# Weight transfers on ScalarE's queue, and moved sums and splits, in a one-core kernel of attention and two MLPs

## The chip, the core and the metric

The program runs on one core of a Trainium2 chip. The metric is the device time of one execution, in microseconds, lower is better. The kernel before was timed three times: median 1686.81 us (1684.53 to 1688.54).

## What is computed

```python
def sm_attn(qq, kk, vv):                         # softmax attention, scale 1/8
    ...
p_packed = sm_attn(p, k, v)                      # p: 32 packed queries a head
out = sm_attn(q, p_packed, p_packed)             # q, k, v: 8 x 8 x 576 x 64
x = out.transpose(0, 2, 1, 3).reshape(4608, 512)
h = x @ w_in1;  x = (h * sigmoid(h)) @ w_out1    # 512 -> 2048 -> 512
h = x @ w_in2;  g = h * clip(h + 3, 0, 6) / 6
out = g @ w_out2                                 # 512 -> 2048 -> 512
```

The two weight pairs arrive as 8-byte floats and are turned into fp32 on the core.

## The kernel before, in words

**Blocks.** The 4608 tokens go through attention and the first MLP in nine blocks (`block`, j = 0 to 8) of 512 columns. A block has 16 steps f, one for each 128 hidden units. In step f TensorE makes `hidden` (12 matmuls in block 0), ScalarE applies Silu (L828) and rounds the result to `gh` (L835), VectorE takes the rest `gl` (L836): every fp32 factor is a sum of a high and a low part, and a product is three matmuls. Then `projects(f - 2)` adds 12 matmuls. Attention for later blocks is spread between these matmuls by `Plan`, which releases a step when its place and its waiting time have come. Every engine runs its list strictly in order.

**Block 0 and `Feed`.** Block 0 also converts the weights of the first MLP. There are 32 pieces (keys), 16 of w_in and 16 of w_out in turn, two for each step f. `advance` number i does, in this order: one `load` (L1215, `load_raw`, L143: a 512 KB transfer into one of four `raw` buffers), `keep()` (stores of finished pieces to DRAM), `conv_end` of key i - 2 (ScalarE's cast L195 makes the high part, L196 the low one: VectorE for w_in, GpSimd for w_out), `conv_add` of key i - 1 (GpSimd, L182) and `conv_bits` of key i (VectorE, L176 and L177). `begin` (ScalarE, L170 and L171, tile `cr`) needs the piece's transfer to have landed. In block 0 `advance` runs after `split_g` and after `projects`, `begin` in the middle of `hidden` and of `projects`. Since an `advance` loads one piece, in block 0 the piece that `advance` i loads is key i + 1, and the `begin` that follows is the one of key i + 1.

**Who issues transfers.** SyncE (SP) issues the loads of k, q, v, p and `raw` in program order; an issue waits until the buffer is free. ScalarE issues the stores of pieces (L189) and the later loads of pieces: `next_in` (L216), `next_out` (L228) and `Prep` (L257, L301 to L303). An issue on ScalarE that has to wait holds up all that stands behind it there. Each transfer uses one of eight semaphores (DMAHW0 to 7), and its issue waits for the transfer that had that one before.

**`Prep`** converts the second MLP's weights in blocks 1 to 8, a piece of work at each call of `step`. Only block 1's first call starts it.

**The second MLP** (`Second`) works on six groups of 768 columns with a scheme of seven products in place of eight. `hidden` makes products k of hidden pieces f; `after` adds them (`hu` L1020, `hv` L1023); `gate` (L1007) makes g. For every odd f, `t1` (L1077, VectorE) and `split` follow 3 and 4 products later; `split` is ScalarE's rounding L1099 and VectorE's rest L1100. `project` runs 28 steps of 12 matmuls; `split` and `sums` prepare coming steps, and `next(self.prep)` does the sums and splits of the next group's x (`x_steps`) at even steps from 4. Weights come from DRAM through a ring of `WS` = 7 buffers `ws` (L942), loaded by SP.

Of the kernel before, what the change touches and what calls it, by code (L numbers as in the profile page):

```python
# [8 lines left out]
F32 = mybir.dt.float32  # L9
I32 = mybir.dt.int32  # L10
U32 = mybir.dt.uint32
F32R = mybir.dt.float32r
# [6 lines left out]
def tile_pack_attention_two_mlps(ctx: ExitStack, tc, q, k, v, p, w_in1, w_out1, w_in2, w_out2, out):  # L19
# [8 lines left out]
    nc = tc.nc  # L28
# [102 lines left out]
    WO = 3  # L131
    made = {}
    raws = {}
    kept = []

    def half_w(kind, f):
        if kind == "in":
# [4 lines left out]

    def load_raw(key, src):  # L143
        raw = wp.tile([P, 2 * T], I32, tag="raw", name="raw", bufs=RAW)
        nc.sync.dma_start(out=raw.rearrange("p (a f) -> p a f", a=src.shape[1]), in_=src)
        raws[key] = raw

    def win_src(w, f):
# [42 lines left out]
    def conv_end(key):  # L191
        kind, f = key
        v = raws.pop(key)
        w = half_w(kind, f)
        nc.scalar.copy(out=w[:, 0], in_=v)  # L195
        (nc.vector if kind == "in" else nc.gpsimd).tensor_sub(out=w[:, 1], in0=v, in1=f32(w[:, 0]))  # L196
        made[key] = w
        if kind == "in":
            kept.append((piece_in(f), f32(w).rearrange("p n (c f) -> p n c f", c=KC)))
        elif f % 2:  # L200
            kept.append((w1o[f].rearrange("n p f -> p n f"), f32(w)))

    def piece_in(f):
        return w1i[f // GF][:, :, :, f % GF, :].rearrange("c p n f -> p n c f")
# [13 lines left out]
                nc.scalar.dma_start(out=f32(t).rearrange("p n (c f) -> p n c f", c=KC), in_=piece_in(key[1]))  # L218
            have_in[key] = t

    projected = [-1]

    def next_out():

        while want_out and not kept and projected[0] >= NF - 2 and (want_out[0][0] * NF + want_out[0][1]) // 2 <= (projected[0] + 1) // 2 - 1 + WO:
            j, f = want_out.pop(0)
            t = half_w("out", f)
            nc.scalar.dma_start(out=f32(t), in_=w1o[f].rearrange("n p f -> p n f"))  # L228
            have_out[j, f] = t
# [7 lines left out]
    class Prep:  # L237
# [28 lines left out]

        def all(self):
            self.load(0)
            yield
            for u, (kind, f, h) in enumerate(self.units):  # L270
                key = "p", u
                c = self.pool.tile([P, 8, P], F32, tag="c8", name="c8")
                hi = self.pool.tile([P, S7, P], F32, tag="hi7", name="hi7")
                conv_begin(key, self.room)
                yield
                yield
                conv_bits(key)
                yield
                if u + 1 < len(self.units):
                    self.load(u + 1)  # L280
                yield
                x, r = (t.rearrange("p (n r f) -> p n r f", n=2, r=2) for t in raws.pop(key))
                a = c[:, 0:4].bitcast(I32)
                a = a.rearrange("p (n r) f -> p n r f", n=2) if kind == "in" else a.rearrange("p (r n) f -> p n r f", n=2)
                nc.gpsimd.tensor_add(out=a, in0=x, in1=r)
                yield

                nc.vector.tensor_add(out=c[:, 4], in0=c[:, 2], in1=c[:, 3])
                nc.vector.tensor_sub(out=c[:, 6], in0=c[:, 0], in1=c[:, 2])
                nc.vector.tensor_sub(out=c[:, 5], in0=c[:, 4], in1=c[:, 0])  # L290
                nc.vector.tensor_sub(out=c[:, 7], in0=c[:, 1], in1=c[:, 5])
                yield
                nc.scalar.copy(out=hi[:, 0:2].bitcast(F32R), in_=c[:, 0:2])
                nc.scalar.copy(out=hi[:, 2:7].bitcast(F32R), in_=c[:, 3:8])
                yield
                nc.gpsimd.tensor_sub(out=c[:, 0:2].bitcast(F32R), in0=c[:, 0:2], in1=hi[:, 0:2])
                nc.gpsimd.tensor_sub(out=c[:, 3:8].bitcast(F32R), in0=c[:, 3:8], in1=hi[:, 2:7])
                yield
                yield
                to = w2[kind][f].rearrange("s p f -> p s f")  # L300
                nc.scalar.dma_start(out=to[:, :, h * P:(h + 1) * P], in_=hi)  # L301
                nc.scalar.dma_start(out=to[:, 0:2, (2 + h) * P:(3 + h) * P], in_=c[:, 0:2])
                nc.scalar.dma_start(out=to[:, 2:7, (2 + h) * P:(3 + h) * P], in_=c[:, 3:8])  # L303
# [602 lines left out]
    ROW = {1: 0, 2: 1, 4: 2, 5: 3, 6: 4, 7: 5, 3: 6}  # L906
    ORDER_P = (1, 5, 6, 3, 7, 2, 4)
    FD = HF // 2
    WS = 7

    class Second:
        def __init__(self):
# [40 lines left out]
        def x_steps(self, n):  # L953

            xr = self.right.tile([P, KC, 2 * N], F32, tag="xr", name="xr")
            at_, end = 2 * N * n, 2 * N * (n + 1)
            o = 0
            while at_ < end:
                j, c0 = divmod(at_, T)
                m = min(end - at_, T - c0)  # L960
                nc.sync.dma_start(out=xr[:, :, o:o + m], in_=x1d[j][:, :, c0:c0 + m].rearrange("c p t -> p c t"))
                at_, o = at_ + m, o + m
            yield
            b = {(i, k): xr[:, 2 * i:2 * i + 2, k * N:(k + 1) * N] for i in range(2) for k in range(2)}
            e = [self.right.tile([P, 2, N], F32, tag=f"xe{i}", name=f"xe{i}") for i in range(3)]
            nc.vector.tensor_sub(out=e[0], in0=b[1, 1], in1=b[0, 1])
            nc.vector.tensor_sub(out=b[0, 1], in0=b[0, 1], in1=b[0, 0])
            yield
            nc.vector.tensor_sub(out=e[1], in0=b[1, 1], in1=b[0, 1])
            nc.vector.tensor_sub(out=e[2], in0=b[1, 0], in1=e[1])  # L970
            yield
            for k, v in (1, b[0, 0]), (6, e[1]), (5, b[0, 1]), (7, e[0]), (2, b[1, 0]), (4, e[2]), (3, b[1, 1]):
                t = self.right.tile([P, 2, 2, N], F32R, tag=f"xc{k}", name=f"xc{k}")
                nc.scalar.copy(out=t[:, 0], in_=v)
                nc.vector.tensor_sub(out=t[:, 1], in0=v, in1=f32(t[:, 0]))
                self.x[k] = t
                yield
# [10 lines left out]
        def hidden(self, n):  # L988
# [25 lines left out]
            def after(f, k):  # L1014
                if k == 1:
                    h1[f] = small("h1")
                    nc.scalar.copy(out=h1[f], in_=X[f])
                elif k == 6:
                    hu[f] = small("hu")
                    nc.vector.tensor_add(out=hu[f], in0=h1[f], in1=Y[f])  # L1020
                elif k == 7:
                    hv[f] = small("hv")
                    nc.vector.tensor_add(out=hv[f], in0=h1[f], in1=Y[f])  # L1023
                    nc.vector.tensor_add(out=hv[f], in0=hv[f], in1=Z[f])
                    act(f, (1, 1), hv[f])
                elif k == 2:
                    act(f, (0, 0), X[f])
                elif k == 4:
                    nc.vector.tensor_add(out=h1[f], in0=h1[f], in1=Y[f])
                    act(f, (1, 0), h1[f])  # L1030
                elif k == 3:
                    nc.vector.tensor_add(out=hu[f], in0=hu[f], in1=Z[f])
                    act(f, (0, 1), hu[f])
                    if f % 2:
                        soon(3, lambda: self.t1(f // 2))
                        soon(4, lambda: self.split(f // 2))

            for fd in range(FD):
                for part in ((0, 0), (0, 1), (1, 0), (1, 1)):
# [43 lines left out]
        def sums(self, s):  # L1083
# [8 lines left out]
            elif k == 4:  # L1092
                nc.vector.tensor_sub(out=t, in0=b21, in1=t)

        def split(self, s):
            if s < FD * S7:
                t = self.left.tile([P, 2, 2, N], F32R, tag="ro", name="ro", bufs=4)
                v = self.operand(s)
                nc.scalar.copy(out=t[:, 0], in_=v)  # L1099
                nc.vector.tensor_sub(out=t[:, 1], in0=v, in1=f32(t[:, 0]))  # L1100
                self.ro[s] = t

        def project(self, n):
            X, Y, Z = [], [], []
# [21 lines left out]
            for s in range(FD * S7):  # L1126
# [15 lines left out]
                self.sums(s + 4)  # L1142
                if s + 3 >= FD:
                    self.split(s + 3)
                if self.prep and s % 2 == 0 and s >= 4:
                    next(self.prep, None)
                yield
            if self.prep:
# [41 lines left out]
    class Feed:  # L1190
# [19 lines left out]
        def advance(self):  # L1210

            i, n = self.at, len(self.keys)
            if i > n + 1:
                return
            if self.loaded < i + self.ahead:  # L1215
                self.load()
            keep()
            if i >= 2:
                conv_end(self.keys[i - 2])
            if 1 <= i <= n:  # L1220
                conv_add(self.keys[i - 1])
            if self.begun == i:
                self.begin()
            if i < n:
                conv_bits(self.keys[i])
            self.at += 1
# [94 lines left out]
    for j in range(NBLK):  # L1321
# [44 lines left out]
        def nxt(f, full, j=j):  # L1366
            if j == 0:
                if full:
                    feed.advance()
                    calls[0] += 1  # L1370
                    if 12 <= calls[0] < 16:
                        next_in()
                else:
                    feed.begin()
            else:
                if j >= B - 1 or full:
                    prep.step()
                if full and j == B:
                    mlp2.begin_step()
# [52 lines left out]
```

## Time and profile before

| what | us |
|---|---|
| median of three runs | 1686.81 |
| the profiled execution's own time | 1691.33 |
| its span, first to last instruction | 1689.5 |
| TensorE (matmuls) busy | 1570.1 (93%) |
| VectorE busy | 1039.1 (62%) |
| ScalarE busy | 804.9 (48%) |
| GpSimd busy | 216.8 (13%) |

The profile is of one execution, 4.5 us longer than the median. An engine's busy time does not say that it sets the pace: a queue can be blocked without being busy, and issuing a transfer is not counted as busy. So a stage is read from what its engines wait for. "gh" rows (L835) mark the steps f of a block, since there is one of them in each step. A row of the timeline gives start, duration, engine, line, operation, output and inputs; in brackets how long the engine had been idle and what ended it. SPq and ACTq are the issues of transfers on SP and ScalarE. A row of windows gives the window and its length, then the busy time of PE, PEld (weight loads), DVE, ACT and POOL with the count of instructions, the granted clock of TensorE, the busy share of the DMA engines and GB/s. A row of waits gives the waiting instruction, what ended its wait, the us in total, the number of waits and the longest.

### The profile page before, as it was taken

What the parts mean: (1) busy time and instruction counts of PE and PEld (TensorE: products, weight loads), DVE (VectorE), ACT (ScalarE), POOL (GpSimd) and SP (SyncE); (2) the same over time, 40 slices, a digit from 0 to 9 for tenths busy, and PEclk for the clock granted to TensorE, in tenths of its full rate; (3) what the DMA queues carried; (4) which work ended last, traced back from release to release, by engine and by line L of the source; (5) the groups of instructions that cost most, each with busy time, mean ns of one, the idle gap of its engine ahead of it and who ended that gap; (6) DMA issues with size and microseconds to landing.
All of it is one profiled execution on the core that took longest, in us unless ns stands there. A gap on an engine that the chain in (4) does not pass through costs nothing.

```text
span 1689.5 us, 23588 instructions
## 1 busy us (share of the span) xinstructions
PE 1570.1 (93%) x8396; PEld 1343.7 (80%) x8396; DVE 1039.1 (62%) x1750; ACT 804.9 (48%) x1356; POOL 216.8 (13%) x188
## 2 busy tenths in 40 slices
PE   5877899889999899999989999999999999999997
PEld 3655656667676677767868999999999999999997
DVE  5645455465556555554343479569578678677675
ACT  4756345555555455555444345345345344444443
POOL 2443311111111021112213000000000000000000
PEclk9999899899999899999999999999999999999999
DMA  7786676776769665766698687787787887887875
GB/s 192 239 254 192 217 213 184 220 209 187 194 181 242 190 195 139 208 218 204 191 311 250 195 274 243 253 294 249 252 294 249 260 286 249 274 271 251 257 252 154
DMA packets 409749, 388.01 MB, mean 230 GB/s; under 512 B 156192, under 2 KB 282144, under 8 KB 409632
## 3 DMA queue, kind: packets, MB, share of 16 engines
q1 hardware_dynamic: 271264, 252.25, 49.6%
q10 hardware_dynamic: 138368, 134.24, 25.6%
q8 instruction: 68, 1.11, 0.3%
q14 instruction: 49, 0.40, 0.1%
HBM read 324.53 MB, written 61.87 MB: 229 GB/s over the span
## 4 chain that ended last, share of the span: by engine, by line
PE 55%; DVE 16%; ACT 13%; DMA 8%; issue 3%; POOL 2%; ACTq 1%; SPq 1%; DVEq 0%; POOLq 0%
PE acc L843 5%; PE b L1137 5%; PE acc L844 5%; PE b L1138 5%; PE acc L845 5%; PE b L1136 5%; PE b L1058 4%; PE b L1060 4%; PE b L1059 4%; PE hps L820 3%; ACT hr L1004 3%; DVE g L1007 3%; PE hps L822 3%; PE hps L821 3%; DVE ro L1100 2%
## 5 line engine op out<-in xcount | busy, mean ns | idle before, releaser
L1058 PE MATMUL b<-xc,ws 128*128 128x384 f32 x672 | 229.4, 341 | 8.0 <-DVE hu L1020 8.0
L1137 PE MATMUL b<-ro,ws 128*128 128x384 f32 x672 | 227.1, 338 | 6.2 <-DVE ro L1100 6.2
L1138 PE MATMUL b<-ro,ws 128*128 128x384 f32 x672 | 225.9, 336 | 0.0
L1136 PE MATMUL b<-ro,ws 128*128 128x384 f32 x672 | 225.8, 336 | 0.0
L1060 PE MATMUL b<-xc,ws 128*128 128x384 f32 x672 | 225.1, 335 | 0.0
L1059 PE MATMUL b<-xc,ws 128*128 128x384 f32 x672 | 224.8, 335 | 0.0
L836 DVE TENSOR_TENSOR gl<-hps,gh 128x512 fp32r<-128x512 f32 x144 | 99.1, 688 | 201.0 <-ACT gh L835 201.0
L1099 ACT CAST ro<-g 128x768 fp32r<-128x768 f32 x168 | 137.3, 835 | 116.9 <-DVE g L1089 34.9
L1100 DVE TENSOR_TENSOR ro<-g,ro 128x768 fp32r<-128x768 f32 x168 | 158.0, 953 | 23.7 <-ACT ro L1099 21.0
L1058 PEld LDWEIGHTS b<-xc,ws 128*128 128x128 f32 x672 | 126.2, 188 | 13.5 <-DVE hu L1020 13.4
L1137 PEld LDWEIGHTS b<-ro,ws 128*128 128x128 f32 x672 | 126.3, 188 | 9.7 <-DVE ro L1100 9.7
L828 ACT ACTIVATE hps<-hps 128x512 f32<-128x512 f32 x144 | 84.1, 584 | 95.6 <-PE hps L822 70.2
L1059 PEld LDWEIGHTS b<-xc,ws 128*128 128x128 f32 x672 | 126.3, 188 | 0.0
L1138 PEld LDWEIGHTS b<-ro,ws 128*128 128x128 f32 x672 | 126.3, 188 | 0.0
L1136 PEld LDWEIGHTS b<-ro,ws 128*128 128x128 f32 x672 | 126.3, 188 | 0.0
L1060 PEld LDWEIGHTS b<-xc,ws 128*128 128x128 f32 x672 | 126.1, 188 | 0.0
L843 PE MATMUL acc<-gh,wr 128*128 128x512 f32 x288 | 120.5, 418 | 0.9 <-ACT gh L835 0.9
L843 PE MATMUL acc<-gh,wo 128*128 128x512 f32 x288 | 117.9, 409 | 2.9 <-ACT gh L835 2.9
L844 PE MATMUL acc<-gl,wr 128*128 128x512 f32 x288 | 115.3, 400 | 0.3 <-DVE gl L836 0.2
L844 PE MATMUL acc<-gl,wo 128*128 128x512 f32 x288 | 114.2, 397 | 0.9 <-DVE gl L836 0.8
L845 PE MATMUL acc<-gh,wr 128*128 128x512 f32 x288 | 114.6, 398 | 0.0
L845 PE MATMUL acc<-gh,wo 128*128 128x512 f32 x288 | 113.8, 395 | 0.0
(262 smaller groups left out, 3046.3 us busy)
## 6 DMA issues: line engine op xcount, KB each, us to landing
ws<-w2in SPq DMA_DIRECT2D x336, 256.0 KB, 3.9
ws<-w2out SPq DMA_DIRECT2D x336, 256.0 KB, 3.5
wi<-w1i ACTq DMA_DIRECT2D x80, 512.0 KB, 4.8
wo<-w1o ACTq DMA_DIRECT2D x64, 512.0 KB, 4.7
x1d<-x SPq DMA_DIRECT2D x18, 512.0 KB, 3.2
raw<-in_moe_w_in_dram SPq DMA_DIRECT2D x16, 512.0 KB, 5.2
raw<-in_moe_w_out_dram SPq DMA_DIRECT2D x16, 512.0 KB, 4.7
w1i<-win ACTq DMA_DIRECT2D x16, 512.0 KB, 5.3
```

What stands on the lines that cost most here:

```text
L836: nc.vector.tensor_sub(out=gl, in0=g, in1=f32(gh))
L843: mm(acc[e], lhsT=w[:, 0, s], rhs=gh, start=first, stop=False)
L844: mm(acc[e], lhsT=w[:, 0, s], rhs=gl, start=False, stop=False)
L845: mm(acc[e], lhsT=w[:, 1, s], rhs=gh, start=False, stop=last)
L1058: mm(ps, lhsT=wh, rhs=xs[k][:, 0, c], start=first, stop=False, skip_group_check=True)
L1059: mm(ps, lhsT=wh, rhs=xs[k][:, 1, c], start=False, stop=False, skip_group_check=True)
L1060: mm(ps, lhsT=wl, rhs=xs[k][:, 0, c], start=False, stop=last, skip_group_check=True)
L1099: nc.scalar.copy(out=t[:, 0], in_=v)
L1100: nc.vector.tensor_sub(out=t[:, 1], in0=v, in1=f32(t[:, 0]))
L1136: mm(acc[i], lhsT=wh, rhs=ro[:, 0, f], start=first, stop=False, skip_group_check=True)
L1137: mm(acc[i], lhsT=wh, rhs=ro[:, 1, f], start=False, stop=False, skip_group_check=True)
L1138: mm(acc[i], lhsT=wl, rhs=ro[:, 0, f], start=False, stop=last, skip_group_check=True)
```

## The change

1. `load_raw` issues on SP only while `early` holds (the part ahead of block 0, five pieces); the other 27 pieces are issued on ScalarE.
2. The low part of a w_in piece (VectorE) is made one `advance` later from i = 6 on.
3. In block 0 `next_in` runs at calls 20 to 23 of `advance` instead of 12 to 15.
4. `next_out` goes by what held at its previous call, so its loads come one step f later.
5. `Prep` begins five calls later, and its tile `hi7` has two buffers.
6. In the second MLP the ring has `WS` = 6 buffers; `t1`, the rounding and the rest follow 2, 3 and 5 products after the odd f; the sums of x are spread over two more steps, and `next(self.prep)` runs at steps 1 to 3, 8 to 11, 16 to 19 and 24 to 27.

```diff
 def load_raw(key, src):
-        nc.sync.dma_start(out=raw..., in_=src)
+        (nc.sync if early[0] else nc.scalar).dma_start(out=raw..., in_=src)
...
 def conv_end(key):
         nc.scalar.copy(out=w[:, 0], in_=v)
-        (nc.vector if kind == "in" else nc.gpsimd).tensor_sub(out=w[:, 1], in0=v, in1=f32(w[:, 0]))
         made[key] = w
         if kind == "in":
-            kept.append((piece_in(f), ...))
-        elif f % 2:
-            kept.append((w1o[f]..., f32(w)))
+            lows.append((v, w, piece_in(f)))
+        else:
+            nc.gpsimd.tensor_sub(out=w[:, 1], in0=v, in1=f32(w[:, 0]))
+            if f % 2:
+                kept.append((w1o[f]..., f32(w)))
+
+    def conv_low():
+        while lows:
+            v, w, to = lows.pop(0)
+            nc.vector.tensor_sub(out=w[:, 1], in0=v, in1=f32(w[:, 0]))
+            kept.append((to, ...))
...
-    projected = [-1]
+    projected = [-1, -1]
 def next_out():
-        while want_out and not kept and projected[0] >= NF - 2 and ... <= (projected[0] + 1) // 2 - 1 + WO:
+        now, projected[1] = projected[1], -1 if kept else projected[0]
+        while want_out and now >= NF - 2 and ... <= (now + 1) // 2 - 1 + WO:
...
 class Prep: def all(self):
             self.load(0)
-            yield
+            for _ in range(6):
+                yield
...
-                hi = self.pool.tile([P, S7, P], F32, tag="hi7", name="hi7")
+                hi = self.pool.tile([P, S7, P], F32, tag="hi7", name="hi7", bufs=2)
...
-    WS = 7
+    WS = 6
...
 def x_steps(self, n):
             nc.vector.tensor_sub(out=e[0], in0=b[1, 1], in1=b[0, 1])
+            yield
             nc.vector.tensor_sub(out=b[0, 1], in0=b[0, 1], in1=b[0, 0])
             yield
             nc.vector.tensor_sub(out=e[1], in0=b[1, 1], in1=b[0, 1])
+            yield
             nc.vector.tensor_sub(out=e[2], in0=b[1, 0], in1=e[1])
...
-                        soon(3, lambda: self.t1(f // 2))
-                        soon(4, lambda: self.split(f // 2))
+                        soon(2, lambda: self.t1(f // 2))
+                        soon(3, lambda: self.split_hi(f // 2))
+                        soon(5, lambda: self.split_lo(f // 2))
...
-                if self.prep and s % 2 == 0 and s >= 4:
+                if self.prep and s and s // FD % 2 == 0:
                     next(self.prep, None)
...
 class Feed: def advance(self):
             if i >= 2:
-                conv_end(self.keys[i - 2])
+                if i < 6:
+                    conv_end(self.keys[i - 2])
+                    conv_low()
+                else:
+                    conv_low()
+                    conv_end(self.keys[i - 2])
...
-                    if 12 <= calls[0] < 16:
+                    if 20 <= calls[0] < 24:
                         next_in()
```

`split_hi` is ScalarE's rounding and `split_lo` VectorE's rest, out of the former `split`, which still calls both.

**How instructions move.** Place 1: ScalarE in block 0, step f = 3, from Silu on (`raw` the arriving piece, `win`, `wo` the converted ones, `cr` L170 and L171 the first part of `begin`). Before:

```order
L828 ACTIVATE hps<-hps 128x512 [waits PE_49]
L835 CAST gh<-hps 128x512 [waits Activation_49]
L189 DMA w1i_109<-win 256x4x128 [waits DMAHW4_49]
L195 CAST wo<-cr 128x512 [waits Pool_49]
L170 ACTIVATE cr<-raw 128x512 [waits DMAHW0_49]
L171 ACTIVATE cr<-raw 128x512
L189 DMA w1i_110<-win 256x4x128 [waits DVE_49]
L195 CAST win<-cr 128x512 [waits DMAHW6_49,Pool_49]
L170 ACTIVATE cr<-raw 128x512 [waits DMAHW2_49]
L171 ACTIVATE cr<-raw 128x512 [waits Activation_49]
```

With the change (lines below `load_raw` have moved: L828 is L838, L835 is L845):

```order
L838 ACTIVATE hps<-hps 128x512 [waits PE_49]
L845 CAST gh<-hps 128x512 [waits Activation_49]
L145 DMA raw<-in_moe_w_in_dram 128x4x256 [waits DMAHW2_49]
L195 CAST wo<-cr 128x512 [waits Pool_49]
L170 ACTIVATE cr<-raw 128x512 [waits DMAHW2_49]
L171 ACTIVATE cr<-raw 128x512
L145 DMA raw<-in_moe_w_out_dram 128x1024 [waits DMAHW3_49,DVE_49]
L189 DMA w1i_109<-win 256x4x128 [waits DMAHW5_49]
L189 DMA w1i_110<-win 256x4x128 [waits DVE_49]
L195 CAST win<-cr 128x512 [waits Pool_49]
L170 ACTIVATE cr<-raw 128x512 [waits DMAHW3_49]
L171 ACTIVATE cr<-raw 128x512 [waits Activation_49]
```

The issue of a `raw` now stands one cast ahead of the L170 that waits for the same semaphore (DMAHW2, DMAHW3); before, no `raw` was issued here, and the L170 waited for pieces that SP had issued.

Place 2: VectorE in the second MLP's `hidden`, after the products of f = 5 (`g` the gated results, `hu`, `hv` sums of products, `ro` the split ones). Before:

```order
L1023 TENSOR_TENSOR hv<-h_8671,b 128x384 [waits PE_49]
L1024 TENSOR_TENSOR hv<-hv,b 128x384 [waits DVE_49]
L1007 SCALAR_TENSOR_TENSOR g_8381<-hr,hv 128x384 [waits DMAHW2_49,Activation_49]
L1077 TENSOR_TENSOR g_8375<-g_8375,g_8374 128x768
L1100 TENSOR_TENSOR ro<-g_8374,ro 128x768 [waits DMAHW3_49,Activation_49]
L1007 SCALAR_TENSOR_TENSOR g_8378<-hr,b 128x384
L1020 TENSOR_TENSOR hu<-h_8749,b 128x384 [waits PE_49]
L1029 TENSOR_TENSOR h_8671<-h_8671,b 128x384 [waits PE_49]
```

With the change (L1024 is L1036, L1077 is L1090, L1007 is L1019, L1020 is L1032, L1100 is L1115):

```order
L1035 TENSOR_TENSOR hv<-h_8668,b 128x384 [waits PE_49]
L1036 TENSOR_TENSOR hv<-hv,b 128x384 [waits DVE_49]
L1090 TENSOR_TENSOR g_8372<-g_8372,g_8371 128x768
L1019 SCALAR_TENSOR_TENSOR g_8378<-hr,hv 128x384 [waits DMAHW6_49,Activation_49]
L1019 SCALAR_TENSOR_TENSOR g_8375<-hr,b 128x384 [waits Activation_49]
L1032 TENSOR_TENSOR hu<-h_8747,b 128x384 [waits PE_49]
L1115 TENSOR_TENSOR ro<-g_8371,ro 128x768 [waits DMAHW2_49]
L1041 TENSOR_TENSOR h_8668<-h_8668,b 128x384 [waits PE_49]
```

`t1` moved ahead of the gate that waits for ScalarE, and the 768-wide rest `ro` moved behind the sum `hu`.

Place 3: ScalarE at the start of block 1 (`wo` pieces of w_out, `praw` raw pieces for `Prep`). Before:

```order
L828 ACT_TABLE_LOAD
L828 ACTIVATE hps<-hps 128x512 [waits PE_49]
L228 DMA wo<-w1o_113 128x2x512 [waits DMAHW5_49]
L228 DMA wo<-w1o_114 128x2x512 [waits DMAHW6_49,DMAHW4_49]
L228 DMA wo<-w1o_115 128x2x512 [waits DMAHW7_49,DMAHW2_49]
L835 CAST gh<-hps 128x512 [waits Activation_49]
L257 DMA praw<-in_moe_w_in_dram 128x2x256 [waits DMAHW3_49,DMAHW0_49]
L257 DMA praw<-in_moe_w_in_dram 128x2x256 [waits DMAHW1_49]
L170 ACTIVATE pr<-praw 128x512 [waits DMAHW1_49,DMAHW0_49]
```

With the change (L228 is L237, L257 is L266, L216 is L224):

```order
L838 ACTIVATE hps<-hps 128x512 [waits PE_49]
L845 CAST gh<-hps 128x512 [waits Activation_49]
L266 DMA praw<-in_moe_w_in_dram 128x2x256 [waits DMAHW5_49,DMAHW3_49,DMAHW0_49]
L266 DMA praw<-in_moe_w_in_dram 128x2x256 [waits DMAHW6_49]
L625 CAST fused<-abank 128x512 [waits PE_49]
L224 DMA wi<-w1i_111 128x1024 [waits DMAHW7_49]
L224 DMA wi<-w1i_111 128x1024 [waits DMAHW1_49]
L838 ACTIVATE hps<-hps 128x512
L237 DMA wo<-w1o_113 128x2x512 [waits DMAHW2_49]
L237 DMA wo<-w1o_114 128x2x512 [waits DMAHW4_49,DMAHW3_49]
L237 DMA wo<-w1o_115 128x2x512 [waits DMAHW4_49]
L845 CAST gh<-hps 128x512 [waits Activation_49]
```

The three loads of `wo` moved from ahead of the first `gh` to ahead of the second, and the L170 of `Prep` is gone from here.

## Rows read from the trace of the kernel before

**Rows 1.** Windows: block 0, blocks 1 to 8, second MLP (columns as told above).
```profile
44.00:200.00 156.00, 125.67 (x593) 92.28 (x593) 89.86 (x129) 94.20 (x168) 66.70 (x49) 0.92 0.74 224
200.00:950.00 750.00, 701.43 (x3482) 528.65 (x3481) 385.67 (x769) 371.83 (x640) 127.44 (x119) 0.97 0.72 207
950.00:1690.00 740.00, 716.62 (x4137) 706.45 (x4135) 538.50 (x795) 320.39 (x511) 14.18 (x6) 1.00 0.79 256
```

**Rows 2.** Waits of ScalarE in block 0: us in total, times, longest.
```profile
ACT win L195 <- POOL cr L182: 22.0, 12, 3.2
...
ACT cr L170 <- DMA raw<-in_moe_w_out_dram: 7.6, 2, 5.2
ACT cr L170 <- DMA wi<-w1i: 7.5, 1, 7.5
ACT cr L170 <- DMA raw<-in_moe_w_in_dram: 6.5, 1, 6.5
```

**Rows 3.** Timeline, block 0: k issues on SP, a raw issue, ScalarE's wait.
```profile
111.04 10.09 SPq L334 DMA_DIRECT2D nat<-in_k_dram  x8
...
121.24 0.96 SPq L145 DMA_DIRECT2D raw<-in_moe_w_in_dram  x1
...
127.62 0.66 ACT L170 ACTIVATE cr<-raw 128x512 f32<-128x512 f32 x1 [6.50 <-DMA raw<-in_moe_w_in_dram]
```

**Rows 4.** Timeline of ScalarE in block 0: begin, step f = 2's gh, exps, f = 13's gh.
```profile
62.38 0.67 ACT L170 ACTIVATE cr<-raw 128x512 f32<-128x512 f32 x1
...
63.52 0.56 ACT L101 COPY T<-abank 128x512 f32<-128x512 f32 x1
...
65.45 0.63 ACT L828 ACTIVATE hps<-hps 128x512 f32<-128x512 f32 x1
66.11 0.58 ACT L835 CAST gh<-hps 128x512 fp32r<-128x512 f32 x1
...
139.43 1.28 ACT L418 ACT_TABLE_LOAD   x1
140.72 0.78 ACT L418 ACTIVATE d<-d,s1m 128x576 f32<-128x576 f32 x1
...
175.10 0.58 ACT L835 CAST gh<-hps 128x512 fp32r<-128x512 f32 x1
```

**Rows 5.** Line 145, issue to landing: window 40:200, then those of 131.2, of 135.0.
```profile
DMA to landing us min/median/max: 3.1/4.9/8.7
...
DMA to landing us min/median/max: 4.3/4.3/4.3
...
DMA to landing us min/median/max: 4.7/4.7/4.7
```

**Rows 6.** Timeline, start of block 1: ScalarE's and TensorE's waits.
```profile
204.46 0.58 ACT L835 CAST gh<-hps 128x512 fp32r<-128x512 f32 x1 [4.85 <-DMA w1o<-wo]
...
205.92 0.66 PE L365 MATMUL abank<-ident,pbd 128*128 128x128 f32 x2 [4.62 <-DVE gl L836]
...
210.19 0.67 ACT L170 ACTIVATE pr<-praw 128x512 f32<-128x512 f32 x1 [5.14 <-DMA praw<-in_moe_w_in_dram]
...
215.54 0.81 PE L399 MATMUL abank<-T,kp 128*64 128x512 f32 x1 [3.15 <-DVE T L385]
```

**Rows 7.** Timeline, start of block 2: TensorE's wait.
```profile
326.01 0.79 PE L820 MATMUL hps<-a2h,fused 128*128 128x512 f32 x1 [3.00 <-DVE gl L836]
```

**Rows 8.** Waits of TensorE in the second MLP.
```profile
PE b L1058 <- DVE hu L1020: 8.0, 12, 1.0
PE b L1137 <- DVE ro L1100: 6.2, 11, 0.8
```

**Rows 9.** Timeline of VectorE in the second MLP's hidden, ahead of a wait.
```profile
996.25 0.56 DVE L1007 SCALAR_TENSOR_TENSOR g<-hr,hv 128x384 f32<-128x384 f32 x1 [0.74 <-ACT hr L1004]
996.73 0.95 DVE L1077 TENSOR_TENSOR g<-g,g 128x768 f32<-128x768 f32 x1
```

**Rows 10.** Line 942, the ring's loads, from issue to landing in the second MLP.
```profile
DMA to landing us min/median/max: 2.5/3.7/9.8
```

More of the change, by code (lines that the diff above doesn't have):

```diff
@@ L133, in tile_pack_attention_two_mlps @@
     raws = {}
-    kept = []
+    kept, lows = [], []
     def half_w(kind, f):
@@ L144, in load_raw @@
         raw = wp.tile([P, 2 * T], I32, tag="raw", name="raw", bufs=RAW)
-        nc.sync.dma_start(out=raw.rearrange("p (a f) -> p a f", a=src.shape[1]), in_=src)
+        (nc.sync if early[0] else nc.scalar).dma_start(out=raw.rearrange("p (a f) -> p a f", a=src.shape[1]), in_=src)
         raws[key] = raw
@@ L195, in conv_end @@
         nc.scalar.copy(out=w[:, 0], in_=v)
-        (nc.vector if kind == "in" else nc.gpsimd).tensor_sub(out=w[:, 1], in0=v, in1=f32(w[:, 0]))
         made[key] = w
         if kind == "in":
-            kept.append((piece_in(f), f32(w).rearrange("p n (c f) -> p n c f", c=KC)))
-        elif f % 2:
-            kept.append((w1o[f].rearrange("n p f -> p n f"), f32(w)))
+            lows.append((v, w, piece_in(f)))
+        else:
+            nc.gpsimd.tensor_sub(out=w[:, 1], in0=v, in1=f32(w[:, 0]))
+            if f % 2:
+                kept.append((w1o[f].rearrange("n p f -> p n f"), f32(w)))
+    def conv_low():
+        while lows:
+            v, w, to = lows.pop(0)
+            nc.vector.tensor_sub(out=w[:, 1], in0=v, in1=f32(w[:, 0]))
+            kept.append((to, f32(w).rearrange("p n (c f) -> p n c f", c=KC)))
     def piece_in(f):
@@ L219, in next_in @@
             have_in[key] = t
-    projected = [-1]
+    projected = [-1, -1]
     def next_out():
-        while want_out and not kept and projected[0] >= NF - 2 and (want_out[0][0] * NF + want_out[0][1]) // 2 <= (projected[0] + 1) // 2 - 1 + WO:
+        now, projected[1] = projected[1], -1 if kept else projected[0]
+        while want_out and now >= NF - 2 and (want_out[0][0] * NF + want_out[0][1]) // 2 <= (now + 1) // 2 - 1 + WO:
             j, f = want_out.pop(0)
@@ L1093, in sums, with split_hi, split_lo @@
                 nc.vector.tensor_sub(out=t, in0=b21, in1=t)
+        def split_hi(self, s):
+            t = self.left.tile([P, 2, 2, N], F32R, tag="ro", name="ro", bufs=4)
+            nc.scalar.copy(out=t[:, 0], in_=self.operand(s))
+            self.ro[s] = t
+        def split_lo(self, s):
+            t = self.ro[s]
+            nc.vector.tensor_sub(out=t[:, 1], in0=self.operand(s), in1=f32(t[:, 0]))
         def split(self, s):
             if s < FD * S7:
[L1097 to L1101, printed above, removed]
+                self.split_hi(s)
+                self.split_lo(s)
         def project(self, n):
```

## The prediction

> **What bounds the kernel now.** I read three views, in this order: the windows, the waits of the engine that is late in each window, and the timeline around the waits that the change touches.
>
> The windows [rows 1] split the span. In blocks 1 to 8 TensorE is busy for 701.43 of 750 us and in the second MLP for 716.62 of 740: what an edit can give there is bounded by TensorE's idle time, 48.6 and 23.4 us. Block 0 is another kind of stage. There TensorE is busy for 125.67 of 156 us at a granted clock of 0.92, VectorE and ScalarE for 90 and 94 us, GpSimd for 67. No engine is full, so something in order sets the pace, and it is ScalarE's list: every piece of weights passes its L170, L171 and L195, between the Silu and the rounding that TensorE waits for. The waits [rows 2] say what holds it up: 22.0 us for GpSimd in front of L195, twelve times, and 21.6 us (7.6 + 7.5 + 6.5) in front of L170 for transfers. The reader is to see in [rows 3] how one of these comes about: SP issues eight loads of k, which takes 10.09 us, the `raw` behind them is only issued at 121.24, and ScalarE's L170 starts at 127.62 after 6.50 us of nothing. But this happened four times in 27 pieces, no more: SP has no other work in its way and issues a `raw` as soon as one of four buffers is free, up to three `advance`s ahead of the L170 that needs it. In all other steps the flight of a piece costs nothing now.
>
> Steps are counted by their gh rows. From f = 2 (66.11) to f = 13 (175.10) eleven steps take 109.0 us, 9.9 us each, stalls included [rows 4].
>
> **Raw loads on ScalarE (part 1).** This edit decides. `advance` i loads key i + 1, and the very next `begin` is that of key i + 1. Place 1 shows the outcome: between the issue on ScalarE and the L170 that waits for the same semaphore stands one cast, L195. Four buffers still exist, but a list in order can't use them: the issue can no longer run ahead of ScalarE's own work. So each piece's time from issue to landing, call it d, lies open on the path, twice per step, and it also hides what used to be paid apart (L195 and its wait for GpSimd run inside d).
>
> The step is then the chain issue, d, L170, L171, issue, d, L170, L171, Silu, gh, issue. Its fixed part comes from [rows 4]: L170 and L171 together take 63.52 - 62.38 = 1.14 us; after the first piece the next issue follows once L171 has started, half of that, 0.57; after the second piece comes all of it, 1.14; Silu to gh is 66.11 - 65.45 = 0.66. Sum 2.37 us.
>
> For d the trace has line 145's own flights [rows 5]: 3.1 to 8.7 us, median 4.9, and single ones, in stretches where no k, q or v was in flight, of 4.3 (a piece of w_in) and 4.7 (of w_out). I take these two, 2d = 9.0, since most of block 0 is such a stretch. The step is 11.37 us, eleven are 125.1 us. Added is what ScalarE does between the pieces and nothing hides: four table loads of 1.28 and three exponentials of some 0.78, 7.5 us [rows 4]; and of the copies out of PSUM (0.56 each) that stand behind an L171 some seven, 4 us. That makes 136.6 us in place of 109.0, +27.6. The steps outside of f = 2 to 13 add about 2 (their loads are partly early ones), and four collisions with k, q and v, which now overtake the `raw`s on their own queue, 1 us each more than the flights alone, another 4. **Block 0: +34 us.** Bounds: with 2d = 7.3 and no collision 106.4 + 11.5 - 109.0 = +9; with 2d = 11.3 (the median 4.9 and a crowded 6.4) 162 in place of 136.6, so about +58. TensorE has the room: its 125.67 us fit into a block of 190. TensorE would then pause in every step, and the granted clock may fall below the 0.92 of [rows 1]; no row here prices that, and it is left to the upper bound.
>
> The Trainium skill, "DMA: Bandwidth & Descriptors", section "Anatomy of one DMA — SWDGE (gpsimd) path", gives a fixed cost of about 2.0 us and bytes at 436 GB/s on top; an estimate from it for these 512 KB is 3.2 us, and by it the eleven steps would take 11 x 8.77 + 11.5 = 108 us, block 0 about the same as now. It was measured on GpSimd's path; here the fastest flight of all, 3.1, agrees with it and the median, 4.9, doesn't [rows 5].
>
> **w_in's low part later, next_in later (parts 2, 3).** Nothing. The low part of a piece for step f + 2 is needed a whole step later, and VectorE, with 90 of 156 us busy, has room. The loads of `wi` for block 1 move eight calls on, still inside block 0, ahead of their use. Bounds -2 (one of the stalls of [rows 2], 7.5 us, has such a `wi` as its releaser; it goes, but the step is then set by d) to +2.
>
> **Block 1's and block 2's starts (parts 4, 5).** Place 3: the three loads of `wo` stand ahead of the first gh now and wait there for the stores of `w1o`; gh is 4.85 us late, and TensorE waits 4.62 for the gl that follows. Then `Prep`'s first L170 waits 5.14 us for its own `praw`, issued just before, and TensorE waits 3.15 behind it [rows 6]. Both leave this place: the loads stand behind gh, the L170 comes five calls later, when its piece has landed. Some of it comes back, since the chain of attention behind it is also in order: **-6**, bounds -7.8 (both whole) and 0. Block 2's start loses a wait of 3.00 us of the same making [rows 7]: **-3**, bounds -3 and +2 (the loads are one step closer to their use). `hi7`'s second buffer and `Prep`'s later start cost nothing: 294 of some 300 steps are used. That all waits in blocks 1 to 8 shift: 0, bounds -8 and +8, by the largest of these waits.
>
> **Second MLP (part 6).** TensorE's waits on VectorE are small: 8.0 us for hu and 6.2 for ro [rows 8]. The place of the first is in [rows 9] and place 2: the gate waits 0.74 us for ScalarE, then the 768-wide t1 (0.95) and the equally wide ro stand ahead of hu. With the change t1 fills the gap of 0.74 and ro goes behind hu, so all of the 8.0 goes; of ro's 6.2 the six waits at the start of `project` stay and the five in `hidden` (some 0.32 each) go, 1.6. Against that stands the ring of six: with a chunk used in some 2.1 us (12 matmuls) a load is issued 10.5 us ahead in place of 12.6, and the flights are 2.5 to 9.8, median 3.7 [rows 10]. The median is far within, the longest only 0.7 us; I take +1.6, bounds 0 and +12 (six groups, each losing one 2.1 us chunk). **Second MLP: -8**, bounds -9.6 and +3.
>
> **Sum.** +34 - 6 - 3 - 8 = +17. The profiled execution took 1691.33 us, so this gives 1708 for it; it lies 4.5 above the median of 1686.81, and taken off that gives **1704 us** against the median, +1.0%.
>
> **Rivals.**
>
> *Flights are short when alone* (chance 0.24). With `raw`s on ScalarE and k, q, v on SP, a `raw` never queues behind SP, and its flight may be nearer to the shortest seen, 3.1, than to 4.3 to 4.7. Then the path is partly that of GpSimd again. At 2d = 7.4 block 0 costs +12 and the sum is -5, 1682; with 3.1 for all block 0 is about 0, the sum -17, 1670. It decides at 2d = 7.9: 29.6 (without collisions) less 11 x 1.15 is the 17 us that the other parts give. For it: the shortest flights in [rows 5]. Against: the median of 4.9, which includes many moments without k, q, v. (The estimate from the Trainium skill's "DMA: Bandwidth & Descriptors" above would be this case at its end of 1670.)
>
> *ScalarE also waits for semaphores at its issues* (0.13). Each issue waits for the transfer that last held its semaphore, and the eight are shared with SP's k, q and v. A group of eight issues lasts 10.09 us [rows 3], and if an issue of ScalarE stands behind each of three such groups of block 0 with everything else behind it, that is +30 in place of the collisions' +4: +43, 1730. For it: place 1 has issues that wait for a semaphore. Against: those are of old transfers, long landed.
>
> *It washes out* (0.10). Between the two, 2d near 7.9, or a larger gain in blocks 1 to 8: 1683.5 to 1690, within 0.2%, about what a measurement of this kernel can tell from no change.
>
> The forecast, 0.53, is slower, and around it 1691 to 1722 by 2d from 7.9 to 10.5.
>
> **How the numbers follow.** Faster 0.24 from the first rival, same 0.10, slower 0.53 + 0.13 = 0.66. The range leaves out the end of the first rival (all flights at 3.1) and the worst of the second: 1675 to 1733.
>
> **What would show it.** In the changed profile ScalarE's waits in front of L170 for `raw` should come to 60 to 90 us, some 25 times, in place of 14.1 us, three times; from f = 2's gh to f = 13's should be about 137 us; line 145's flights, now on ScalarE, should have a median near 4.5. TensorE should show no wait of 4.62 or 3.15 at block 1's start and almost none for hu in the second MLP, with ro near 4.6. Wrong would be: L195's waits for GpSimd still near 22 us and L170's few (the flights are hidden, first rival), issues on ScalarE that last 5 us or more (second), or waits of TensorE for `ws` in the second MLP of over 5 us (the ring).

## The result, and the profile after

The changed kernel takes 1706.66 us (median of four, 1698.97 to 1709.23) against 1687.67 for the kernel before: 1.0108 times its time, 95% interval 1.0072 to 1.0144. It is slower, by 18 us (12 to 24).

The profiled execution is the shortest of the four, 1698.97 us, with a span of 1697.2; the one before was 4.5 above its median. So the two traces differ by 7.7 us only, and what the three longer executions lost beyond that, no trace shows. The traces are used for where time moves, the medians for how much.

Windows of the changed kernel, block 0 and second MLP, to be held against [rows 1]:

```profile
44.00:200.00 156.00, 113.74 (x517) 79.06 (x515) 91.35 (x116) 86.45 (x155) 63.44 (x46) 0.86 0.71 206
...
950.00:1690.00 740.00, 729.19 (x4214) 720.24 (x4212) 541.85 (x802) 324.35 (x517) 14.46 (x6) 1.00 0.80 258
```

In the window of block 0 TensorE now has 517 matmuls done where it had 593, at a granted clock of 0.86 in place of 0.92 (no run separates what the lower clock costs); in the last window it has 4214 in place of 4137. The block fell behind, the second MLP caught some of it up. Three gh rows (L845 now) date it, those of f = 2, 13 and 15 of block 0:

```profile
69.25 0.58 ACT L845 CAST gh<-hps 128x512 fp32r<-128x512 f32 x1
...
190.43 0.59 ACT L845 CAST gh<-hps 128x512 fp32r<-128x512 f32 x1
...
204.70 0.59 ACT L845 CAST gh<-hps 128x512 fp32r<-128x512 f32 x1
```

and of the kernel before that of f = 15:

```profile
187.04 0.59 ACT L835 CAST gh<-hps 128x512 fp32r<-128x512 f32 x1
```

From f = 2 to f = 13 it is 121.2 us (190.43 - 69.25) where [rows 4] had 109.0; at f = 15 the changed kernel is 17.7 us late. Why is in the waits of ScalarE, window 40:240 (total, times, longest):

```profile
ACT cr L170 <- DMA raw<-in_moe_w_in_dram: 28.0, 10, 4.8
ACT cr L170 <- DMA raw<-in_moe_w_out_dram: 24.1, 13, 3.8
ACT win L195 <- POOL cr L182: 6.6, 3, 3.1
```

L170 waits for a `raw` 23 times, 52.1 us in all, in place of three times, 14.1; L195's wait for GpSimd, 22.0 us in [rows 2], is down to 6.6 because it runs inside a flight. The chain that sets the block's end names the same. First its shares by line in the kernel before (60 to 187 us), then in the changed one (60 to 204 us):

```profile
by line: issue 10.2%; DMA wi<-w1i 9.5%; POOL cr L182 8.2%; SPq L334 6.4%; DMA nat<-in_k_dram 6.4%; DMA raw<-in_moe_w_out_dram 6.2%; DMA raw<-in_moe_w_in_dram 5.0%; ACT cr L171 4.7%; POOL wo L196 4.5%; ACT cr L170 4.2%; PE hps L820 2.3%; PE 
```

```profile
by line: DMA raw<-in_moe_w_out_dram 28.4%; DMA raw<-in_moe_w_in_dram 24.5%; DMA qt<-in_q_dram 5.6%; ACT cr L170 5.1%; ACT cr L171 4.1%; ACT hps L838 3.9%; DVE win L208 3.7%; issue 3.3%; PE hps L832 2.9%; PE hps L830 2.2%; PE hps L831 1.7%; 
```

Flights of `raw` were 11.2% of a mixed chain; now they are 52.9% of it, 76 of 144 us. One step of that chain, start and duration:

```profile
122.53 4.03 DMA raw<-in_moe_w_in_dram
126.59 3.83 DMA raw<-in_moe_w_out_dram
130.44 0.68 ACT cr L170
131.12 0.55 ACT cr L171
131.67 0.49 ACT hps L838
132.19 5.16 DMA raw<-in_moe_w_in_dram
```

From one issue (122.53) to the next of the same kind (132.19) a step takes 9.66 us, of which 4.03 + 3.83 are flights. On ScalarE the same step shows when the second issue goes out, as the first L170 starts:

```profile
126.58 0.68 ACT L170 ACTIVATE cr<-raw 128x512 f32<-128x512 f32 x1 [2.47 <-DMA raw<-in_moe_w_in_dram]
126.59 0.35 ACTq L145 DMA_DIRECT2D raw<-in_moe_w_out_dram  x1
```

The second MLP, from the last gh of block 8 to the end, takes 746.3 us in place of 753.9. TensorE's waits there, for [rows 8]:

```profile
PE b L1156 <- DVE ro L1115: 6.2, 6, 1.0
PE b L1071 <- DVE hv L1035: 2.4, 7, 0.4
PE b L1071 <- DVE hu L1032: 0.6, 2, 0.3
```

The waits for hu are down from 8.0 to 0.6, some (2.4) are now for hv, and those for ro are 6.2 still, in six waits in place of eleven. No wait for a `ws` appears: the ring of six holds.

One row of the changed trace the prediction had not asked for. TensorE's waits for the late low part, block 0:

```profile
PE hps L832 <- DVE win L208: 30.9, 13, 8.2
```

### The profile page after: what moved, and what is told of

Its sections match the earlier page's. It is cut to its first block, busy times and chain, and to the rows that moved or that the text cites. A ratio compares the mean times of both kernels' runs of the same rounds, so it can differ in the third digit from the quotient of the medians.

```text
span 1697.2 us, 23539 instructions
## 1 busy us (share of the span) xinstructions
PE 1567.1 (92%) x8396; PEld 1339.9 (79%) x8396; DVE 1049.2 (62%) x1750; ACT 806.8 (48%) x1356; POOL 219.3 (13%) x188
## 4 chain that ended last, share of the span: by engine, by line
PE 54%; DVE 16%; ACT 13%; DMA 11%; issue 3%; ACTq 2%; SPq 1%; POOL 0%; DVEq 0%; POOLq 0%
PE b L1156 6%; PE b L1157 6%; PE b L1155 6%; PE acc L853 5%; PE acc L854 5%; PE acc L855 5%; ACT hr L1016 4%; DVE g L1019 4%; PE hps L830 3%; PE hps L832 3%; DMA raw<-in_moe_w_out_dram 3%; PE hps L831 3%; PE b L1073 2%; PE b L1071 2%; PE b L1072 2%
## 5 line engine op out<-in xcount | busy, mean ns | idle before, releaser
L1115 DVE TENSOR_TENSOR ro<-g,ro 128x768 fp32r<-128x768 f32 x168 | 158.5, 951 | 9.1 <-ACT ro L1110 7.7
L838 ACT ACTIVATE hps<-hps 128x512 f32<-128x512 f32 x144 | 84.0, 583 | 95.2 <-PE hps L832 77.1
```

What stands on the lines that cost most here:

```text
L1115: nc.vector.tensor_sub(out=t[:, 1], in0=self.operand(s), in1=f32(t[:, 0]))
```

## The experiments

Theory 1: the `raw` loads on ScalarE cost the time, since an issue placed one cast ahead of its use lays the flight open (part 1). Theory 2: the late low part of w_in costs it (part 2), by the 30.9 us just shown. Each run was timed beside the kernel before on the same chip; ratios are to that.

| run | median us | ratio (95%) | last gh of block 0 | blocks 1 to 8 | second MLP |
|---|---|---|---|---|---|
| before | 1686.5 to 1689.2 | 1 | 187.0 | 748.5 | 753.9 |
| changed | 1706.66 | 1.0108 (1.0072 to 1.0144) | 204.7 | 746.2 | 746.3 |
| e1 | 1688.04 | 1.0004 (0.9995 to 1.0013) | 189.0 | 748.1 | 746.3 |
| e2 | 1700.39 | 1.0078 (1.0062 to 1.0094) | 206.7 | 744.7 | 746.6 |
| e3 | 1678.51 | 0.9951 (0.9937 to 0.9964) | 181.5 | 748.3 | 746.4 |
| e4 | 1704.47 | 1.0107 (1.0090 to 1.0125) | 202.4 | 751.5 | 753.9 |
| e5 | 1687.30 | 1.0002 (0.9984 to 1.0019) | 189.0 | 746.9 | 746.6 |
| e6 | 1680.62 | 0.9956 (0.9943 to 0.9970) | 183.5 | 746.3 | 746.3 |
| e7 | 1683.61 | 0.9983 (0.9970 to 0.9997) | 180.0 | 744.8 | 754.0 |
| e8 | 1690.60 | 1.0015 (1.0002 to 1.0028) | 182.0 | 750.2 | 754.0 |
| e9 | 1678.64 | 0.9948 (0.9932 to 0.9963) | 182.5 | 748.6 | 746.3 |
| e10 | 1673.47 | 0.9918 (0.9902 to 0.9934) | 175.0 | 748.9 | 746.3 |
| e11 | 1669.50 | 0.9887 (0.9867 to 0.9906) | 172.0 | 750.8 | 746.3 |
| e12 | 1690.59 | 1.0013 (0.9999 to 1.0027) | 185.0 | 752.1 | 753.9 |

The last three columns are of one trace each (last gh of block 0 from the span's start; from it to the last gh of block 8; from that to the end). The second MLP repeats to 0.3 us. Block 0 doesn't: the kernel before, e6, e8 and e12, which do the same there, end it at 187.0, 183.5, 182.0 and 185.0 (mean 184.4), so 5 us of that column are scatter, and blocks 1 to 8 scatter no less.

**e1.** Raw loads back on SP:

```diff
-        (nc.sync if early[0] else nc.scalar).dma_start(out=raw..., in_=src)
+        nc.sync.dma_start(out=raw..., in_=src)
```

> The changed kernel, but all raw loads issued on SP as before; the w_in low part stays one advance later. Theory 1 (open flights: a raw issued on ScalarE one cast ahead of the L170 that needs it lies open twice a step): block 0's last gh falls from 204.7 to 187 to 190 us, ScalarE's L170 waits for raw from 52 us (23 times) to under 20, and the time from 1706.7 to 1680 to 1690. Theory 2 (late low part: TensorE's wait for win's low part, 30.9 us in 13 waits of the changed kernel, is what the block pays): the last gh stays above 200, those waits stay near 30 us, the time stays above 1700.

It took 1688.04 us, 18 below the changed kernel, and block 0 ends at 189.0, as theory 1 said. ScalarE's waits of e1 in block 0:

```profile
ACT win L195 <- POOL cr L182: 22.6, 12, 3.2
ACT cr L170 <- DMA raw<-in_moe_w_in_dram: 10.3, 2, 6.3
ACT cr L170 <- DMA raw<-in_moe_w_out_dram: 7.7, 2, 5.5
```

But theory 2's sign is there too, TensorE's waits for the low part stay:

```profile
PE hps L832 <- DVE win L208: 26.8, 12, 8.6
```

**e2.** The low part at once:

```diff
-                if i < 6:
-                    conv_end(self.keys[i - 2])
-                    conv_low()
-                else:
-                    conv_low()
-                    conv_end(self.keys[i - 2])
+                conv_end(self.keys[i - 2])
+                conv_low()
```

> The changed kernel, but the w_in low part is made in the same advance as the high part, as before; raw loads stay on ScalarE. Theory 1: TensorE's waits for win's low part vanish and nothing comes of it, since the flights run in the same time: last gh of block 0 202 to 206 us, time 1701 to 1708. Theory 2: last gh near 190, time under 1693.

1700.39 us, last gh 206.7, each just outside theory 1's range and far from theory 2's: the 30.9 us of waits are gone and block 0 has not become shorter. With the raw loads on ScalarE those waits ran in the same time as the flights. The medians differ by 6 us, but the intervals of the two ratios overlap, and the traces show no place for a difference.

**e3.** Both edits at once.

> The changed kernel with raw loads on SP and the low part at once: what is left is next_in, next_out and Prep later and the second MLP's edits. Both theories: block 0 as before (last gh 186 to 189 us). By the prediction's terms -3 -6 -8 against before: 1670 to 1680, faster than both kernels. If block 0's loss was a matter of next_in or of the starts, it stays above 1690.

1678.51 us, faster than both kernels. Against e1, which differs in the low part alone, it is 9.5 us less, with intervals apart, and block 0 ends 7.5 us earlier (at 181.5, below the 186 to 189 expected); e1's row first, then e3's:

```profile
188.98 0.59 ACT L845 CAST gh<-hps 128x512 fp32r<-128x512 f32 x1
```

```profile
181.47 0.59 ACT L845 CAST gh<-hps 128x512 fp32r<-128x512 f32 x1
```

So part 2 isn't free: where no flight covers it, it costs 9 us. The two costs lie in parallel: undoing the low part alone (e2) shows nothing, since the flights remain, and undoing the raw loads alone (e1) leaves the low part's cost standing.

**e4.** The kernel before with e1's edit the other way round, raw loads on ScalarE.

> The kernel before with one edit: the 27 raw loads after the early part issued on ScalarE. Theory 1: block 0 alone loses 12 to 18 us (last gh 199 to 206), L170's waits for raw near 50 us, time 1699 to 1706. Theory 2: last gh within 3 us of 187, time within 4 us of 1687.7. The Trainium skill, DMA: Bandwidth & Descriptors, Anatomy of one DMA, would have a flight of 3.2 us (an estimate) and little loss.

1704.47 us, +18.0 by the ratio, last gh 202.4. Part 1 alone makes as much as the whole change. The flights on ScalarE's queue in the changed kernel (issues: minimum, median, maximum in ns, first and last start; then issue to landing):

```profile
L145 ACTq DMA_DIRECT2D raw<-in_moe_w_out_dram x14: 334/347/637, 49.4 to 190.4; - x14
L145 ACTq DMA_DIRECT2D raw<-in_moe_w_in_dram x13: 374/379/432, 48.2 to 180.3; - x13
...
DMA to landing us min/median/max: 3.5/3.9/8.1
```

The Trainium skill's "DMA: Bandwidth & Descriptors", section "Anatomy of one DMA — SWDGE (gpsimd) path", led to an estimate of 3.2 us. The shortest flight here is 3.5, the median 3.9: every flight of the changed kernel is longer than the estimate, and the loss that it made small was 18 us.

**e5.** Is it the engine or the place? The changed kernel, one line changed, so that every issue moves one `begin` ahead and stays on ScalarE:

```diff
 class Feed: def advance(self):
-            if self.loaded < i + self.ahead:
+            while self.loaded < min(i + self.ahead, len(self.keys)):
                 self.load()
```

> The changed kernel with one word: advance loads while, not if, the pieces loaded are fewer than its aim, so that it catches up by one and each raw is issued on ScalarE one begin earlier; still on ScalarE, low part still late. Theory 1 (the place of the issue in ScalarE's order costs, not the engine): L170's waits for raw fall from 52 us to under 20, last gh of block 0 falls from 204.7 to 188 to 192 us, time 1685 to 1692, as with the loads on SP (1688.0). Rival (ScalarE's issues themselves, or the flights next to SP's k, q, v, cost): waits go down but issues on ScalarE wait for semaphores, last gh above 198, time above 1697.

1687.30 us, the same as on SP. Who waited for line 145 at L170 (us, times), and the flights' times:

```profile
  ACT cr L170: 0.4, 1
...
DMA to landing us min/median/max: 3.2/4.7/8.0
```

One wait of 0.4 us is left of 52.1, though the median flight, 4.7, is longer than before. GpSimd's chain is back in front of L195:

```profile
ACT win L195 <- POOL cr L182: 22.1, 12, 3.1
```

The distance between issue and use is the cause of the 18 us, not the queue. This fits a sentence of the Trainium skill ("DMA: Bandwidth & Descriptors", "Issuing engines are not separate DMA queues"): issuing from another engine only saves time on the sequencer; here ScalarE (e5) and SP (e1) are 0.7 us apart.

**e6.** The second MLP's edits alone (part 6 of the change).

> The kernel before with the second MLP's edits alone (ring of 6, t1, rounding and rest at 2, 3 and 5 products, sums of x spread). Prediction's term: -8, of it TensorE's waits for hu 8.0 to about 0 and for ro 6.2 to 4.6, the ring +1.6. From the changed kernel's trace (last gh to the end 746.3 in place of 753.9): time 1678 to 1680. If the gain belonged to what comes before, 1686.

1680.62 us, by the ratio -7.4; the second MLP takes 746.3 us as in the changed kernel. The gain is its own, though the time is 0.6 us above the range expected.

**e7.** Part 3 alone, `next_in` at calls 20 to 23.

> The kernel before with next_in at calls 20 to 23 alone. The prediction put it at nothing, since a flight's stall would only be replaced. With the raw loads on SP, as here, ScalarE's wait of 7.5 us for wi (rows 2) should go: last gh of block 0 187 to 181 to 183 us, time 1681 to 1686. If the wait comes back for another transfer: 1685 to 1688.

1683.61 us, -2.9 (-5.1 to -0.5); block 0 ends at 180.0. The wait of 7.5 us for `wi` [rows 2] is gone. The prediction had let it come back for something else.

**e8.** Parts 4 and 5 alone, without the second `hi7`.

> The kernel before with next_out one step later and Prep five calls later (one hi7 buffer, since the ring of 7 leaves no room for two). Prediction's terms -6 and -3: from last gh of block 0 to first of block 1 17.4 to 11 to 12 us, to block 2's 23.0 to 20 to 21, time 1677 to 1681 if all of it stays. If blocks 1 to 8 give it back (as the low-part run's and the both-back run's stages hint, some 6 us): 1684 to 1687.

1690.60 us, +2.5 (0.3 to 4.7), beyond both expectations. From the last gh of block 0 to the first of block 1 it is 12.6 us in place of 17.4, as meant. But the waits have moved on by one gh. Timeline of e8 in block 1: three issues of `wo` in front of the second gh, that gh, and TensorE, whose wait ends with the gh after that (202.83 to 203.41):

```profile
198.88 2.42 ACTq L229 DMA_DIRECT2D wo<-w1o  x3
...
201.34 0.58 ACT L837 CAST gh<-hps 128x512 fp32r<-128x512 f32 x1 [1.91 <-issue]
...
203.42 2.51 PE L401 MATMUL abank<-T,kp 128*64 128x512 f32 x3 [3.69 <-ACT gh L837]
```

TensorE waits 3.69 us there. In the 133 us from the last gh of block 0 on, its listed waits come to 13.9 us in e8 and to 13.8 in the kernel before: what went at one place came back at others. Block 2 takes 92.4 us from first to last gh where it took 87.5; what makes that longer isn't shown.

**e12.** Part 4 alone, `next_out` one step later.

> The kernel before with next_out one step later alone, Prep as before. From the run of both: the gap from last gh of block 0 to first of block 1 falls by some 5 us (17.0 to 12) and block 2 gets 4 to 5 us longer. If next_out does both: 1688 to 1691. If the loss in block 2 is Prep's, and next_out's gain stays: 1683 to 1685.

1690.59 us, by the ratio +2.2 (-0.2 to 4.6), not told apart from no change. The gap is 12.6 us, but most of the loss sits in block 1, 104.3 us in place of 97.2; block 2 has 90.3 in place of 87.5. Timeline of e12: `Prep`'s issue, its L170, TensorE:

```profile
199.83 0.99 ACTq L258 DMA_DIRECT2D praw<-in_moe_w_in_dram  x2
...
204.36 0.66 ACT L170 ACTIVATE pr<-praw 128x512 f32<-128x512 f32 x1 [6.12 <-DMA praw<-in_moe_w_in_dram]
...
210.12 3.07 PE L400 MATMUL abank<-T,kp 128*64 128x512 f32 x4 [7.38 <-DVE T L386]
```

With `gh` earlier the L170 that waits for its own `praw` comes earlier too, and the landing doesn't: 6.12 us in place of 5.14, and TensorE behind it 7.38 in place of 3.15 [rows 6]. With part 5 (e8) this wait of L170 isn't there, and the time is the same, 1690.60: part 4 gains nothing, alone or with part 5.

**e9, e10, e11.** The kernel before with the parts that gained: `next_in` later and the second MLP's edits (e9); with e5's `while` and the raw loads on ScalarE (e10); with the `while` and the raw loads on SP (e11).

> The kernel before with the two parts that gained alone: next_in at calls 20 to 23 and the second MLP's edits. If the parts add: -3.9 and -6.9 on 1687.5, so 1676 to 1678, faster than both kernels and 1 to 3 us below the both-back run (1678.5), which also had the later next_out and Prep. If the later Prep and next_out were needed for the two: 1680 or more.

> The run with next_in and the second MLP, plus raw loads on ScalarE issued one begin earlier. Theory 1: L170's waits for raw, some 18 us in block 0 with SP, fall to under 5, last gh of block 0 falls by 3 to 6 us to 175 to 179, time 1670 to 1675. Rival: GpSimd's chain in front of L195 (22 us) sets the block once the flights are hidden: last gh as in the next_in run (180), time 1676 to 1678.

> The same with the raw loads one begin earlier but left on SP. If what was missing is distance alone, SP's order moves the raws ahead of the k and v groups too: last gh 175 to 179, time 1670 to 1675 like the run on ScalarE. If SP's order behind k, q and v is what delays a raw: L170's waits stay at 15 us or more and the time at 1676 to 1678.

e9 took 1678.64 us, 8.8 us less than the kernel before, where the parts alone (e6, e7) gave 7.4 + 2.9 = 10.3; that is within the intervals, and the time is 0.6 us above what adding parts had led to expect. e10 took 1673.47, as expected. e11 took **1669.50 us**, 0.9887 of the time before, the shortest of all: faster than the kernel before by 19 us and than the changed one by 37. It is a little better than expected, and its block 0 ends at 172.0 where 175 to 179 stood. ScalarE's waits in block 0, e9 first, then e11:

```profile
ACT win L195 <- POOL cr L182: 22.6, 12, 3.2
ACT cr L170 <- DMA raw<-in_moe_w_in_dram: 10.7, 2, 6.5
ACT cr L170 <- DMA raw<-in_moe_w_out_dram: 10.0, 2, 7.5
```

```profile
ACT win L195 <- POOL cr L182: 21.5, 12, 3.2
...
ACT cr L170 <- DMA raw<-in_moe_w_out_dram: 6.5, 3, 3.2
...
ACT cr L170 <- DMA raw<-in_moe_w_in_dram: 4.7, 1, 4.7
```

One `advance` of distance halves L170's waits, 20.7 to 11.2 us, on SP too, and block 0 ends 10 us earlier. What stays is GpSimd's 21.5 us in front of L195, the next wait to look at in this block. e10 hid the `raw`s wholly, yet is 4 us behind e11; its ScalarE waits at two L195 for transfers that are SP's:

```profile
ACT win L195 <- DMA qt<-in_q_dram: 5.1, 1, 5.1
ACT wr L195 <- DMA nat<-in_v_dram: 3.5, 1, 3.5
```

No such row stands in e11. That this makes the 4 us was not tried by itself.

## Why the prediction was right, and where it was not

The time, 1704 us, was 2.7 from the measured one, and the mechanism named as decisive is the one that the runs show. The sum behind it held less well: two terms were wrong by much, in opposite senses (block 0 some 16 us too much loss, the block starts 11.5 us too much gain). That the time came out within 2.7 us is luck.

- **Block 0, +34: right in cause, too large.** The trace has +17.7 (+20.3 against the mean of the four that do as before there), e4's median +18.0 for the raw loads alone. The sign that was asked for (25 waits, 60 to 90 us) came as 23 waits and 52.1 us. From f = 2 to f = 13, 136.6 us were forecast and 121.2 measured, 15.4 less. The flights were nearly right: from an issue of `raw` to the L170 that uses it, the eleven steps take 95.9 us, 8.7 a step (8.5 without the one step in which `qt` is in the way), where 2d = 9.0 made 99. Of the 37.6 us taken for all the rest (11 x 2.37, and 7.5 + 4 for what stands between the pieces) only 25.3 came. First, the fixed part: it was taken as 2.37 us, and in the step shown above it is 9.66 - 7.86 = 1.80, since the second issue goes out as the first L170 starts (126.59), not once L171 has started. Second, "nothing hides" failed: two of the four table loads and all three exponentials of these steps run inside a flight. In the step from 89.02 on, the L170 behind them shows no idle time before it:

```profile
89.02 0.38 ACTq L145 DMA_DIRECT2D raw<-in_moe_w_in_dram  x1
89.61 1.28 ACT L428 ACT_TABLE_LOAD   x1
90.90 0.78 ACT L428 ACTIVATE d<-d,s1m 128x576 f32<-128x576 f32 x1
...
92.84 0.69 ACT L170 ACTIVATE cr<-raw 128x512 f32<-128x512 f32 x1
```

- **The low part later, nothing: wrong, though it didn't show here.** The step said that hidden of f + 2 needs it, "a whole step later". The rows of the changed kernel say otherwise: gl at 123.14, the low part behind it on VectorE, and TensorE's L832 right after, waiting:

```profile
123.14 0.69 DVE L846 TENSOR_TENSOR gl<-hps,gh 128x512 fp32r<-128x512 f32 x1 [4.82 <-ACT gh L845]
...
123.70 1.28 POOL L200 TENSOR_TENSOR wo<-cr,wo 128x512 fp32r<-128x512 f32 x1 [6.59 <-ACT wo L195]
123.75 1.78 DVE L208 TENSOR_TENSOR win<-cr,win 128x512 fp32r<-128x512 f32 x1
...
125.58 0.79 PE L832 MATMUL hps<-xh,win 128*128 128x512 f32 x1 [0.96 <-DVE win L208]
...
144.76 0.68 DVE L208 TENSOR_TENSOR win<-cr,win 128x512 fp32r<-128x512 f32 x1
...
144.97 1.63 POOL L200 TENSOR_TENSOR wo<-cr,wo 128x512 fp32r<-128x512 f32 x1 [6.29 <-ACT wo L195]
```

  The `hidden` that comes next takes it at once. The cover was named wrongly; the real cover was part 1's flights, and without them (e1 against e3) it costs 9 us.
- **`next_in` later, nothing: too little.** Alone it gains 2.9 us (e7).
- **Block 1's and block 2's starts, -9: wrong.** Both waits went from their places, as foretold, and came back one gh later: alone the two parts cost 2.5 us (e8). The step that failed is "both leave this place", read as a gain: it priced the waits that go, and didn't follow the three issues to where they now stand, ahead of the next gh.
- **Second MLP, -8: right in size, by terms that weren't.** -7.6 in the trace, -7.4 in e6. But TensorE's waits there fell by 5.0 us (14.2 to 9.2), not by 9.6: ro's total stayed at 6.2 where 4.6 was expected, and 2.4 us of waits for hv are new. The ring, priced at 1.6, cost TensorE no wait. The other 2.6 us are in none of its listed waits, and no run parts the edits of part 6, so where they come from stays open.
- **The rivals.** The first, short flights, needed 2d below 7.9; it came to 8.7 (8.5 without the `qt` step). Its point of balance was wrong all the same, since it rested on a gain of 17 us elsewhere, most of which didn't come. The second, issues of ScalarE held by SP's transfers, did occur, once: a store's issue waits for `qt<-in_q_dram`, and the L195 behind it starts 5.1 us late. Three such places of 10 us were its price.

Adding what stands alone, +18.0 (e4), +2.5 (e8) and -7.4 (e6), makes +13. e2, the change without part 2, bears that out: its ratio lies 4.9 us below e4's, as much as 2.5 - 7.4, so beside open flights `next_in` shows no gain of its own. The measured +18 has an interval from 12 to 24. The remaining 5 us lie between e2 and the changed kernel, where only the low part differs. Their intervals overlap, so whether this is scatter or a part of the low part's cost that the flights don't cover stays open.

## What to carry to other kernels

When a transfer moves to another engine's queue, ask first how far ahead of its use the issue then stands (18 us here), and only then which queue it is (4 us between e10 and e11, cause not tried): count, in that engine's order, what lies between the issue and the instruction that waits for it, and set a flight against it. When a wait is taken from one place of an in-order engine, follow the moved instructions to the place where they now stand, and price the wait there before booking the gain. And undo parts in pairs: two costs that run in the same time hide each other, and neither shows until the other is gone.

## What the runs showed of the hardware

VectorE's low part (128x512) took 0.68 us at 144.76, when it began before GpSimd's L200, and 1.78 at 123.75, when L200 had begun 0.05 us earlier; in the first case it was GpSimd's that got longer, 1.63 in place of 1.28. The later of the two takes about as long as what is left of the first and its own time. The Trainium skill says so of the pair ("SBUF — State Buffer", section "SBUF: two separate sides": an exclusive lock, whoever starts first holds it for the whole instruction), and the trace agrees. Put later in the order, the low part took longer: its mean was 1.50 us, of 12, in the changed kernel between 60 and 200 us, and 1.12, of 13, in the kernel before (60 to 185).
